# A forgetting-attention and feed-forward kernel: TensorE's order in the attention part written out by hand

## The chip, the cores and the metric

One core of one Trainium2 chip runs the whole program. The metric is the device time of one execution in microseconds (us). The kernel before took 1072.08 us, the median of three runs (1070.17 to 1072.96).

## The reference

Attention with a forget gate over 4 batches, 8 heads, 576 positions and 64 columns per head, then two feed-forward blocks over the 2304 tokens:

```python
scores = scale * np.matmul(q, k.transpose(0, 1, 3, 2))
cum = np.cumsum(np.log(np.clip(f, 0.0001, 1.0)), axis=-1)
scores = np.where(causal, -1e9, scores + cum[..., :, None] - cum[..., None, :])
attn = softmax(scores)
x = merge_heads(np.matmul(attn, v))                  # 2304 x 512
h = x @ w_in                                         # 512 -> 2048
x = (h * np.tanh(softplus(h))) @ w_out               # 2048 -> 512
out = ((x @ w1) * (x @ w2)) @ w3 @ w_out2            # 512 -> 1024 -> 1024 -> 512
```

## The kernel before

**Layout.** The 32 heads are worked on as 16 pairs; the two heads of a pair lie on the lower and the upper 64 partitions. The kernel multiplies `w3 @ w_out2` once into one weight (`wp`). Weights come in as 64-bit words and are turned into fp32 by a conversion job: one load (`cv_load`, SP's queue), one ScalarE instruction (`cv_exp`, L127), three VectorE instructions (`cv_bits`, L135 to L137), and then either a split into a high and a low part (`cv_split`: ScalarE L92, GpSimd L106) or a store (`cv_store`). There are 62 such jobs in the slots described below: 14 for w3 (slots 0 to 18), 16 for w_in (from slot 20, one a slot) and 32 for w_out, w1 and w2 (from slot 40). A large product of two split operands takes three matmuls (`MM_PAIRS`).

**One pair.** A pair has 576 query rows, cut into units c = 0 to 4: c = 0 to 3 are 128 rows of both heads against the first 128(c+1) keys, c = 4 is the last 64 rows of both heads together. Per unit:

- `scores` (L339 for c < 4, L344 for c = 4): raw products in fp32 (each matmul appears as two records) plus one product that adds the decay (`aug`). For c < 4 the two heads use 64 rows of the array each and write two different PSUM banks. There are two score buffers, `ps_s`, of two banks each, taken in turn by `bank()`.
- `softmax_a`: VectorE's mask-and-reduce (L363; L369 and L370 for c = 4), then ScalarE's exponential (L373), one of each per head.
- `transposes` (L407, L411, L412) of the exponentials through TensorE into `ps_t`, and `pt_parts` (L422, L425, L426), the copies out: head 0 on ScalarE, head 1 on VectorE.

After the five units of pair p, `pv(p)` (L440) multiplies by V: 28 records, the two heads in the left and the right 64 columns of the array, into a score buffer. The row sums are inverted (`inv_sums`, `inv_rows` with one transpose, L388), stored and read back from DRAM as rows (`inv_load`, tile `R`), and `x_rows` (L448) multiplies the P V result by them; `x_parts` splits it into the two halves that the first layer reads.

**Slots and fillers.** The attention is written as slots, five per pair; slot s issues `scores(s)`, then the transposes of slot s-1 (`T_LAG`), and `pv` of the pair before stands in the third slot of each pair (`PV_AT`). Between them run single matmuls from a queue, the fillers: 192 of `wp` (L481, 128x512), then the first layer (L511, 128x288) of batches 0 to 2, 384 each; `run_filler` takes them in order, as soon as the weights they need are marked in `done`. How many each slot takes is worked out by `plan` from costs given in `slot_cost`, over the stretches `WP_END` and `L1_S`. The first layer of batch 3 and everything after it (L775, L795, L815) is `phase_b`; it has no attention work. All of its matmuls are 128x288.

**What sets the order on the engines.** The program gives dependencies and priorities (`high_priority`); a scheduler that models the engines' time then places every engine's instructions, TensorE's too. `issue_after` adds an order on one engine: each filler goes behind the latest score matmul (`self.pe`), the conversions behind the softmax of their slot. [...]

Of the kernel before, what the change touches and what calls it, by code (L numbers as in the profile page):

```python
# [24 lines left out]
TB = S // 2  # L25
# [8 lines left out]
KQ = 3 * S  # L34
LAST = 2 * S - 64

T_LAG = 1
PV_AT = 2
HB = 3
CV = 2  # L40
HP_L1 = 50
# [4 lines left out]
MID = 7  # L46
EARLY = 10
W3_STEP = 1.42
PRE = 6
WP_END = 28  # L50
W_IN_SLOT = 20
L1_BOTH = 10
W_IN_STEP = 1.0
W_OUT_SLOT = 40
W_OUT_STEP = 1.3
L1_S = (23, 43, 64, 86)

MM_PAIRS = ((0, 0), (0, 1), (1, 0))

# [11 lines left out]
class Kernel:  # L71
# [4 lines left out]
    def __init__(self, ctx, tc, qk, v, f, w_in, w_out, w1, w2, w3t, wo2, out_t):  # L76
        self.ctx, self.tc, self.nc = ctx, tc, tc.nc
        self.qk, self.v, self.f = qk, v, f
        words = [w.bitcast(I32) for w in (w_in, w_out, w1, w2, w3t, wo2)]
        self.w_in, self.w_out, self.w1, self.w2, self.w3t, self.wo2 = words  # L80
        self.out_t = out_t
        self.cv, self.done, self.owed = {}, set(), 0
        self.V = {}
        self.filler = deque()
        self.nl1 = 0
        self.pe = None
# [51 lines left out]

    def cv_split(self, key, hi, lo, hi_eng="act", lo_eng="pool"):
        self.split(self.cv.pop(key)[1], hi, lo, hi_eng, lo_eng)  # L140
        self.done.add(key)

    def cv_store(self, key, dst):
        self.nc.sync.dma_start(dst, self.cv.pop(key)[1])
# [180 lines left out]
        self.V[p] = self.va  # L325


    def scores(self, s):
        p, c = divmod(s, NU)
        mm = self.nc.tensor.matmul  # L330
        ps = self.S[s] = self.bank()
        raw, aug = self.raw[p % 2], self.aug[p % 2]
        if c < 4:
            n = 128 * (c + 1)
            for t, first in ((raw, True), (aug, False)):
                for hh in range(2):
                    r = slice(64 * hh, 64 * hh + 64)
                    q0 = (2 * S + 64 if hh else S) + 128 * c
                    ins = mm(ps[:, 512 * hh:512 * hh + n], t[r, q0:q0 + 128], t[r, 0:n],  # L339
                             start=first, stop=not first)  # L340
            return ins
        for t, first in ((raw, True), (aug, False)):
            for part in range(2):
                ins = mm(ps[:, 512 * part:512 * part + TB], t[:, LAST:LAST + 128], t[:, TB * part:TB * part + TB],  # L344
                         start=first, stop=not first)
        return ins

    def softmax_a(self, s):
        p, c = divmod(s, NU)
        nc = self.nc  # L350
        ps = self.S.pop(s)
        if c == 0:
            self.sums = self.att.tile([128, 16], F32, name=f"sum{p}", tag="sum", bufs=2)
        ttr = nc.vector.tensor_tensor_reduce
        self.nsm = self.nsm % 6 + 1
        st = [self.sums[:, 8 + self.nsm:9 + self.nsm]]
        if c < 4:
            n = 128 * (c + 1)
            P = [self.P[(2 * s + hh) % 4] for hh in range(2)]
            self.nsm = self.nsm % 6 + 1  # L360
            st.append(self.sums[:, 8 + self.nsm:9 + self.nsm])
            for hh in range(2):
                ttr(P[hh][:, :n], ps[:, 512 * hh:512 * hh + n], self.m1[:, 512 - n:], -0.125, 3.0e38, ALU.add,  # L363
                    ALU.min, st[hh])
            cols = (c, 5 + c)
        else:
            n = S
            P = [self.P[2 * s % 4]]
            ttr(P[0][:, :TB], ps[:, :TB], self.m1[:, :TB], -0.125, 3.0e38, ALU.add, ALU.min, self.sums[:, 15:16])  # L369
            ttr(P[0][:, TB:n], ps[:, 512:512 + TB], self.m4, -0.125, self.sums[:, 15:16], ALU.add, ALU.min, st[0])  # L370
            cols = (4,)
        for t, b, i in zip(P, st, cols):
            ins = nc.scalar.activation(t[:, :n], t[:, :n], AF.Exp, bias=b, scale=-1.0, accum_out=self.sums[:, i:i + 1])  # L373
        return ins
# [25 lines left out]
    def transposes(self, s):  # L400
        p, c = divmod(s, NU)
        tr = self.nc.tensor.transpose
        if c < 4:
            for hh in range(2):
                P = self.P[(2 * s + hh) % 4]
                for k in range(c + 1):
                    tr(self.ps_t[hh][:, 128 * k:128 * k + 128], P[:, 128 * k:128 * k + 128], self.ident)  # L407
            return
        P = self.P[2 * s % 4]
# [4 lines left out]
    def pt_parts(self, s, hh):  # L414

        p, c = divmod(s, NU)
        nc = self.nc
        copy = nc.vector.tensor_copy if hh else nc.scalar.copy
        dst = self.pt[:, 2 * (p % 2) + hh]
        if c < 4:  # L420
            src = self.ps_t[hh][:, :128 * (c + 1)].rearrange("p (k q) -> p k q", q=128)
# [115 lines left out]
        return out  # L537


    @staticmethod  # L540
    def slot_cost(s):
        t = 0
        if s < NU * NPAIR:
            c = s % NU
            t += (300, 590, 880, 1170, 1320)[c]
        if 0 <= s - T_LAG < NU * NPAIR:
            t += (220, 440, 660, 880, 470)[(s - T_LAG) % NU]
        if s >= NU and s % NU == PV_AT:
            t += 2950
        return t  # L550

    def run_filler(self, n):

        self.owed += n
        while self.owed and self.filler and all(k in self.done for k in self.filler[0][0]):
            with self.behind(self.pe):
                self.filler.popleft()[1]()
            self.owed -= 1

    def behind(self, ins):  # L560
# [2 lines left out]

    def plan(self):

        last = NU * NPAIR + NU
        cnt = [0] * last
        segs = [(0, WP_END, 8 * 24 - PRE, 231)] + [(L1_S[i], min(L1_S[i + 1], last), 384, 132) for i in range(3)]
        for a, z, n, c in segs:
            cost = [self.slot_cost(s) for s in range(a, z)]  # L570
            lo, hi = 0.0, 1e6
            for _ in range(60):
                t = (lo + hi) / 2
                if sum(max(0.0, t - x) for x in cost) < n * c:
                    lo = t
                else:
                    hi = t
            acc, done = 0.0, 0
            for s, x in zip(range(a, z), cost):
                acc += max(0.0, lo - x) / c  # L580
                k = min(n, int(acc + 0.5)) - done
                cnt[s] = k
                done += k
        return cnt

    def phase_a(self):
# [31 lines left out]
            if i + EARLY < len(first):  # L618
                self.cv_load(first[i + EARLY][0], first[i + EARLY][1], where[i + EARLY])

        for i in range(7):
            go(i)
        self.filler.extend(self.wp_unit(0))
        self.run_filler(PRE)
        for i in range(7, 10):
            go(i)

        misc, conv = {}, {}
# [34 lines left out]
        for f in range(1, 8):  # L663
            self.filler.extend(self.wp_unit(f))
        cnt = self.plan()
        nslot = NU * NPAIR
        self.S, self.nsm = {}, 0
        act = dve = None
        for s in range(nslot + NU):
# [3 lines left out]
            with self.tc.high_priority(offset=HP_ATT):  # L673
                if s < nslot:
                    self.pe = self.scores(s)
                if 0 <= s - T_LAG < nslot:
                    self.transposes(s - T_LAG)
                    act = self.pt_parts(s - T_LAG, 0)
            if s < nslot:
                with self.tc.high_priority(offset=HP_SM):  # L680
                    act = self.softmax_a(s)
            with self.behind(act):
# [4 lines left out]
            if 0 <= s - T_LAG < nslot:  # L687
                with self.tc.high_priority(offset=HP_ATT):
                    dve = self.pt_parts(s - T_LAG, 1)
            with self.behind(dve):  # L690
                for key in conv.get(s, []):
                    self.cv_bits(key)
            with self.behind(act):
                for fn, a in misc.get(s, []):
                    fn(*a)
            self.run_filler(n - k)
            if s >= NU and s % NU == PV_AT:
                with self.tc.high_priority(offset=HP_PV):
                    p = s // NU - 1
                    self.pv(p)  # L700
                    self.x_rows(p)
                    self.x_parts(p)
        self.run_filler(len(self.filler))
        self.psp.__exit__(None, None, None)
        self.attp.__exit__(None, None, None)
        self.lowp.__exit__(None, None, None)


    def late_pool(self):
# [221 lines left out]
```

## Time and profile before

| | |
|---|---|
| median of the runs | 1072.08 us |
| the profiled execution | 1066.5 us |
| its span, first to last instruction | 1064.7 us |
| TensorE matmul busy | 1015.1 us (95%) |
| TensorE weight load busy | 887.2 us (83%) |
| VectorE busy | 420.2 us (39%) |
| ScalarE busy | 374.6 us (35%) |
| GpSimd busy | 232.6 us (22%) |
| mean granted TensorE clock | 0.995 |

The profile is of one execution. A matmul's end is modelled in it, and the next one may start before that end, so the cost of a matmul is read from the start of one to the start of the next, and a busy TensorE need not be a TensorE at its peak. PE is TensorE's matmuls, PEld its weight loads, DVE VectorE, ACT ScalarE, POOL GpSimd, SP the engine whose queue issues all DMAs here. In the timeline a line is a run of like instructions: start, time until the last one's modelled end, engine, line, tile written and read, rows*columns of the array, operand, how many, and in brackets the idle time before it and what ended it.

### The profile page before, as it was taken

The numbers are of one execution on the slowest core, as the hardware profiler recorded it, in microseconds if no ns is written. First come the engines' busy times: TensorE is split into PE (matmuls) and PEld (weight loads), VectorE is DVE, ScalarE is ACT, GpSimd is POOL, SyncE is SP. The second block draws the span as 40 slices with busy tenths as digits, with TensorE's granted clock in tenths as the row PEclk, the third lists the DMA queues.
The fourth block names the chain that finished last, engine by engine and source line by source line (L and its number), as shares of the span: only waits on it lengthen the run. The fifth ranks groups of instructions, "written<-read, shape, count | busy, mean of one in ns | idle before, by whom it ended". The sixth has DMA issues, their size and how long they took to land.

```text
span 1064.7 us, 18244 instructions
## 1 busy us (share of the span) xinstructions
PE 1015.1 (95%) x6912; PEld 887.2 (83%) x6912; DVE 420.2 (39%) x1049; ACT 374.6 (35%) x987; POOL 232.6 (22%) x299
## 2 busy tenths in 40 slices
PE   1698899999999999999999999999999999999998
PEld 0465567767777767669999999999999999999998
DVE  6956565653445455532232222222232122322311
ACT  2655556554355444443453121121212121121111
POOL 4632223320010000001571221212122121222100
PEclk9999999999999999999999999999999999999999
DMA  6545556652665666556973111111112111111000
GB/s 203 159 144 150 163 166 183 191 168 73 200 202 171 192 188 192 172 166 200 358 216 120 47 55 40 45 48 49 56 40 56 35 50 51 46 53 37 12 24 23
DMA packets 101132, 126.27 MB, mean 119 GB/s; under 512 B 10324, under 2 KB 81380, under 8 KB 101044
## 3 DMA queue, kind: packets, MB, share of 16 engines
q1 hardware_dynamic: 101044, 125.10, 39.1%
q8 instruction: 54, 0.88, 0.4%
q14 instruction: 34, 0.28, 0.1%
HBM read 88.43 MB, written 36.54 MB: 117 GB/s over the span
## 4 chain that ended last, share of the span: by engine, by line
PE 85%; DMA 8%; DVE 4%; SPq 1%; ACT 1%; issue 1%; POOL 0%; ACTq 0%; DVEq 0%
PE ps_x L775 18%; PE ps_l L511 17%; PE ps_y L795 10%; PE ps_l L795 10%; PE ps_s L440 6%; PE ps_s L339 5%; PE ps_l L815 5%; PE ps_y L815 5%; PE ps_l L481 3%; PE ps_t L407 3%; DMA cvro<-in_wo_dram 2%; PE ps_s L344 2%; DMA cvri<-in_w_in_dram 1%; DMA R<-inv_scr 1%; DMA cvrt<-in_w3t_dram 1%
## 5 line engine op out<-in xcount | busy, mean ns | idle before, releaser
L511 PE MATMUL ps_l<-x,wi 128*128 128x288 f32 x1536 | 251.3, 306 | 2.6 <-ACT h L518 1.6
L511 PEld LDWEIGHTS ps_l<-x,wi 128*128 128x128 f32 x1536 | 213.2, 189 | 34.6 <-issue 23.6
L775 PE MATMUL ps_x<-g,wo 128*128 128x288 f32 x1536 | 215.4, 294 | 0.0
L775 PEld LDWEIGHTS ps_x<-g,wo 128*128 128x128 f32 x1536 | 207.3, 188 | 0.0
L106 POOL TENSOR_TENSOR g<-m,g 128x288 fp32r<-128x288 f32 x128 | 106.2, 830 | 376.0 <-DVE g L94 362.3
L757 ACT ACTIVATE m<-hl 128x288 f32<-128x288 f32 x128 | 56.9, 446 | 283.1 <-POOL g L106 281.5
L795 PE MATMUL ps_y<-x,w 128*128 128x288 f32 x768 | 106.8, 294 | 0.0
L795 PE MATMUL ps_l<-x,w 128*128 128x288 f32 x768 | 106.7, 294 | 0.0
L795 PEld LDWEIGHTS ps_y<-x,w 128*128 128x128 f32 x768 | 103.3, 188 | 0.0
L795 PEld LDWEIGHTS ps_l<-x,w 128*128 128x128 f32 x768 | 103.3, 188 | 0.0
L373 ACT ACTIVATE P<-P,sum 128x128 f32<-128x128 f32 (+2 forms) x144 | 84.0, 584 | 51.9 <-DVE sum L363 47.1
L363 DVE CUSTOM_DVE_ANT_0 P<-ps_s,m 128x128 f32<-128x128 f32 (+3 forms) x128 | 59.7, 486 | 97.5 <-PE ps_t L407 80.5
L106 POOL TENSOR_TENSOR x<-xx,x 128x288 fp32r<-128x288 f32 x32 | 27.2, 872 | 263.7 <-ACT x L92 208.7
L803 DVE TENSOR_TENSOR cs<-ps_y,cs 128x288 f32<-128x288 f32 x32 | 14.7, 458 | 170.9 <-PE ps_y L795 170.9
L94 DVE CAST g<-m 128x288 fp32r<-128x288 f32 x128 | 41.1, 322 | 101.4 <-PE ps_x L775 97.9
L440 PE MATMUL ps_s<-pt,va 128*64 128x320 f32 (+3 forms) x384 | 77.6, 395 | 0.0
L339 PE MATMUL ps_s<-raw 64*128 64x128 f32 (+3 forms) x256 | 65.6, 497 | 5.9 <-DMA raw<-in_qk_dram 5.2
L407 PE MATMUL ps_t<-ident,P 128*128 128x128 f32 x320 | 58.5, 284 | 2.6 <-DVE pt L422 1.4
L339 PE MATMUL ps_s<-aug 64*128 64x128 f32 (+3 forms) x128 | 40.1, 515 | 21.2 <-DVE cvo L135 21.2
L407 PEld LDWEIGHTS ps_t<-ident,P 128*128 128x128 f32 x320 | 38.1, 141 | 25.7 <-issue 11.5
L518 ACT COPY h<-ps_l 128x288 f32<-128x288 f32 x96 | 37.8, 394 | 54.8 <-PE ps_l L511 33.0
L815 PE MATMUL ps_y<-ab,wpl 128*128 128x288 f32 x384 | 52.1, 294 | 0.0
(117 smaller groups left out, 1114.5 us busy)
## 6 DMA issues: line engine op xcount, KB each, us to landing
hl<-h_scr SPq DMA_DIRECT2D x128, 144.0 KB
h_scr<-h SPq DMA_DIRECT2D x96, 144.0 KB
raw<-in_qk_dram SPq DMA_DIRECT2D x32, 288.0 KB
cvrt<-in_w3t_dram SPq DMA_DIRECT2D x16, 512.0 KB
cvri<-in_w_in_dram SPq DMA_DIRECT2D x16, 512.0 KB
cvru<-in_w_out_dram SPq DMA_DIRECT2D x16, 512.0 KB
cvrv<-in_w_dram SPq DMA_DIRECT2D x16, 512.0 KB
h_scr<-hst SPq DMA_DIRECT2D x32, 144.0 KB
```

What stands on the lines that cost most here:

```text
L94: nc.vector.tensor_copy(hi, raw)
L106: ins = self.nc.gpsimd.tensor_tensor(lo[..., c], raw[..., c], f32(hi[..., c]), ALU.subtract)
L339: ins = mm(ps[:, 512 * hh:512 * hh + n], t[r, q0:q0 + 128], t[r, 0:n], start=first, stop=not first)
L363: ttr(P[hh][:, :n], ps[:, 512 * hh:512 * hh + n], self.m1[:, 512 - n:], -0.125, 3.0e38, ALU.add, ALU.min, st[hh])
L373: ins = nc.scalar.activation(t[:, :n], t[:, :n], AF.Exp, bias=b, scale=-1.0, accum_out=self.sums[:, i:i + 1])
L407: tr(self.ps_t[hh][:, 128 * k:128 * k + 128], P[:, 128 * k:128 * k + 128], self.ident)
L440: mm(ps[64 * hh:64 * hh + 64, 256 + q:256 + q + w], lhs, rhs, start=i == 0, stop=i == len(plan) - 1)
L511: mm(o[:, :TB], w, x, start=i == 0, stop=i == 11)
L757: self.nc.scalar.activation(y, h, AF.Mish)
L775: ins = mm(self.xb(e), self.wo[f][:, 512 * a + 128 * e:512 * a + 128 * e + 128], g[:, TB * b:TB * b + TB], start=f == 0 and k == 0, stop=f ...
L795: mm(ps, self.w12[f, i][:, 512 * a + 128 * e:512 * a + 128 * e + 128], self.x2[e][:, TB * b:TB * b + TB], start=n == 0, stop=n == 11)
L815: nc.tensor.matmul(ps, self.wp[f][:, 512 * a + 128 * e:512 * a + 128 * e + 128], self.ab[f][:, TB * b:TB * b + TB], start=n == 0, stop=n = ...
```

## The change

`T_LAG`, `PV_AT`, `PRE` and `slot_cost` go. In the attention part TensorE's instructions keep the order in which the program writes them (`manual_schedule`); the other engines are still placed by the scheduler. A pair's five slots hold: scores of units 0 and 1; transposes of 0 and 1, then scores of 2 and 3; transposes of 2; transposes of 3, then scores of 4; transposes of 4, then P V of the pair before. Fillers follow in each slot, in two halves with the slot's small jobs between them, in the proportions of `SHARE` (24, 18, 12, 18, 24; 96 in each slot behind the last pair). A weight counts as ready only from the slot after the one that converted it (`fresh`). The steps of the inverted sums move one slot earlier, the six `wp` fillers ahead of the slots go into them, `P` buffers and the columns of `ps_t` are numbered by c, and the stretches of the fillers move.

```diff
-T_LAG = 1
-PV_AT = 2
-PRE = 6
-WP_END = 28
+WP_END = 26
-L1_S = (23, 43, 64, 86)
+L1_S = (26, 46, 66, 84)
+SHARE = (24, 18, 12, 18, 24)
...
     def cv_split(self, key, hi, lo, hi_eng="act", lo_eng="pool"):
         self.split(self.cv.pop(key)[1], hi, lo, hi_eng, lo_eng)
-        self.done.add(key)
+        self.fresh.add(key)
...
-            P = [self.P[(2 * s + hh) % 4] for hh in range(2)]
+            P = [self.P[(2 * c + hh) % 4] for hh in range(2)]
...
-            P = [self.P[2 * s % 4]]
+            P = [self.P[0]]
...
+    def t_col(c):
+        return 128 if c == 1 else 0
...
     def run_filler(self, n):
 
         self.owed += n
         while self.owed and self.filler and all(k in self.done for k in self.filler[0][0]):
-            with self.behind(self.pe):
-                self.filler.popleft()[1]()
+            self.filler.popleft()[1]()
             self.owed -= 1
...
-        segs = [(0, WP_END, 8 * 24 - PRE, 231)] + [(L1_S[i], min(L1_S[i + 1], last), 384, 132) for i in range(3)]
...
+        segs = [(0, WP_END, 8 * 24)] + [(L1_S[i], L1_S[i + 1], 384) for i in range(3)]
+        for a, z, n in segs:
+            share = [SHARE[s % NU] if s < NU * NPAIR else 96 for s in range(a, z)]
             acc, done = 0.0, 0
...
+                acc += n * x / sum(share)
...
-        for i in range(7):
-            go(i)
-        self.filler.extend(self.wp_unit(0))
-        self.run_filler(PRE)
-        for i in range(7, 10):
+        for i in range(10):
             go(i)
...
-            at(s + 4, self.inv_sums)
-            at(s + 5, self.inv_rows, p)
-            at(s + 6, self.inv_load, p)
+            at(s + 3, self.inv_sums)
+            at(s + 4, self.inv_rows, p)
+            at(s + 5, self.inv_load, p)
...
+        with self.tc.manual_schedule(engines={mybir.EngineType.PE}):
+            self.slots(misc, conv, self.plan())
...
+    def slots(self, misc, conv, cnt):
+
+        def turn(p, cs):
+            with self.tc.high_priority(offset=HP_ATT):
+                for c in cs:
+                    self.transposes(p, c)
+                for c in cs:
+                    self.act = self.pt_parts(p, c, 0)
+                    self.dve = self.pt_parts(p, c, 1)
+
+        def score(p, cs):
+            with self.tc.high_priority(offset=HP_SM):
+                for c in cs:
+                    self.scores(p, c)
+                for c in cs:
+                    self.act = self.softmax(p, c)
+
+        for s in range(NU * (NPAIR + 1)):
+            self.done |= self.fresh
+            self.fresh.clear()
             if s in L1_S[:3]:
                 self.filler.extend(self.l1_all(L1_S.index(s)))
+            p, j = divmod(s, NU)
             n = cnt[s]
...
+            live = p < NPAIR
+            if live:
+                if j == 0:
+                    score(p, (0, 1))
+                elif j == 1:
+                    turn(p, (0, 1))
+                    score(p, (2, 3))
+                elif j == 2:
+                    turn(p, (2,))
+                elif j == 3:
+                    turn(p, (3,))
+                    score(p, (4,))
+                else:
+                    turn(p, (4,))
+            if p and j == (4 if live else 2):
+                with self.tc.high_priority(offset=HP_PV):
+                    self.pv(p - 1)
+                    self.x_rows(p - 1)
+                    self.x_parts(p - 1)
+            with self.behind(self.act):
                 for key in conv.get(s, []):
                     self.cv_exp(key)
+            with self.behind(self.dve):
+                for key in conv.get(s, []):
+                    self.cv_bits(key)
             k = n // 2
             self.run_filler(k)
...
+            with self.behind(self.act):
                 for fn, a in misc.get(s, []):
                     fn(*a)
             self.run_filler(n - k)
```

## Rows read from the trace of the kernel before

**Rows 1.** Busy time by stretch: stretch, length, each engine, granted clock, DMA share, GB/s.
```profile
156.50:485.40 328.90, 324.95 (x1993) 236.26 (x1991) 166.50 (x438) 162.63 (x462) 44.59 (x54) 1.00 0.59 178
485.40:1064.70 579.30, 575.10 (x4342) 574.50 (x4341) 147.91 (x369) 132.79 (x328) 128.75 (x159) 1.00 0.24 73
```
**Rows 2.** The same view of line L511 alone (matmuls, weight loads).
```profile
181.20:439.70 258.50, 140.56 (x804) 113.07 (x804) 1.00 0.59 175
0.00:485.40 485.40, 181.15 (x1036) 145.62 (x1036) 0.99 0.58 173
```
**Rows 3.** The same view of line L481 alone.
```profile
50.50:156.50 106.00, 47.24 (x168) 30.21 (x168) 0.97 0.53 157
```
**Rows 4.** Timeline of TensorE, 224 to 226 us: part of one pair's P V.
```profile
224.73 0.75 PE L440 MATMUL ps_s<-pt,va 128*64 128x320 f32 x2
225.41 0.40 PE L511 MATMUL ps_l<-x,wi 128*128 128x288 f32 x1
225.74 0.75 PE L440 MATMUL ps_s<-pt,va 128*64 128x320 f32 x2
```
**Rows 5.** Timeline of TensorE: first and last score and P V piece, 181 to 440 us.
```profile
181.21 0.49 PE L339 MATMUL ps_s<-raw 64*128 64x128 f32 x4
...
192.23 1.41 PE L440 MATMUL ps_s<-pt,va 128*64 128x256 f32 x12
...
432.58 0.33 PE L440 MATMUL ps_s<-pt,vb 128*64 128x64 f32 x2
...
434.12 1.13 PE L339 MATMUL ps_s<-raw 64*128 64x512 f32 x4
```
**Rows 6.** Timeline of TensorE, 77 to 97 us: groups that run undivided, and what follows.
```profile
77.29 0.71 PE L407 MATMUL ps_t<-ident,P 128*128 128x128 f32 x5
77.83 1.14 PE L344 MATMUL ps_s<-raw 128*128 128x288 f32 x4
...
79.06 0.61 PE L481 MATMUL ps_l<-wo,w3h 128*128 128x512 f32 x2
...
80.51 0.49 PE L339 MATMUL ps_s<-raw 64*128 64x128 f32 x4
...
81.00 0.73 PE L481 MATMUL ps_l<-wo,w3h 128*128 128x512 f32 x2
...
90.99 1.30 PE L440 MATMUL ps_s<-pt,va 128*64 128x320 f32 x8
92.22 0.28 PE L388 MATMUL ps_t<-ident,sum 128*9 128x128 f32 x1
...
95.67 1.13 PE L339 MATMUL ps_s<-raw 64*128 64x512 f32 x4
...
96.96 0.73 PE L481 MATMUL ps_l<-wo,w3h 128*128 128x512 f32 x2
```
**Rows 7.** Timeline of TensorE, 60 to 62 us: three L481 matmuls in a row.
```profile
60.76 0.62 PE L481 MATMUL ps_l<-wo,w3h 128*128 128x512 f32 x2
...
61.44 0.62 PE L481 MATMUL ps_l<-wo,w3h 128*128 128x512 f32 x2
```
**Rows 8.** Timeline of TensorE, 50 to 54 us: pair 1 begins, and a wait.
```profile
50.49 0.49 PE L339 MATMUL ps_s<-raw 64*128 64x128 f32 x4
...
53.85 1.02 PE L481 MATMUL ps_l<-wo,w3h 128*128 128x512 f32 x2 [2.33 <-ACT w3h L92]
```
**Rows 9.** Groups by line and form, 181.2 to 439.7 us: busy us, mean ns, idle before.
```profile
L373 ACT ACTIVATE P<-P,sum 128x256 f32<-128x256 f32 x18 | 9.0, 504 | 0.7 <-DVE sum L363 0.7
...
L137 DVE SCALAR_TENSOR_TENSOR cvi<-cvri,cvi 128x512 int32<-128x512 int32 x10 | 7.9, 788 | 0.2
...
L363 DVE CUSTOM_DVE_ANT_0 P<-ps_s,m 128x256 f32<-128x256 f32 x18 | 6.9, 421 | 6.6 <-PE ps_t L411 5.1 <-PE ps_s L339 1.4
```
**Rows 10.** Timeline of TensorE at 102 us: a wait for the row factors.
```profile
102.01 2.29 PE L344 MATMUL ps_s<-raw 128*128 128x288 f32 x4 [3.17 <-DVE xx L448]
```
**Rows 11.** Waits, 50 to 485 us: engine, line, waited for: total us, times, longest us.
```profile
ACT cvi L127 <- DMA cvri<-in_w_in_dram: 10.9, 8, 2.7
```

More of the change, by code (lines that the diff above doesn't have):

```diff
@@ L81, in __init__ @@
         self.out_t = out_t
-        self.cv, self.done, self.owed = {}, set(), 0
+        self.cv, self.done, self.fresh, self.owed = {}, set(), set(), 0
         self.V = {}
@@ L325, in load_v, with scores @@
         self.V[p] = self.va
-    def scores(self, s):
-        p, c = divmod(s, NU)
+    def scores(self, p, c):
         mm = self.nc.tensor.matmul
-        ps = self.S[s] = self.bank()
+        ps = self.S[p, c] = self.bank()
         raw, aug = self.raw[p % 2], self.aug[p % 2]
@@ L338, in scores, with softmax @@
                     q0 = (2 * S + 64 if hh else S) + 128 * c
-                    ins = mm(ps[:, 512 * hh:512 * hh + n], t[r, q0:q0 + 128], t[r, 0:n],
-                             start=first, stop=not first)
-            return ins
+                    mm(ps[:, 512 * hh:512 * hh + n], t[r, q0:q0 + 128], t[r, 0:n], start=first, stop=not first)
+            return
         for t, first in ((raw, True), (aug, False)):
             for part in range(2):
[L344 to L349, printed above, removed]
+                mm(ps[:, 512 * part:512 * part + TB], t[:, LAST:LAST + 128], t[:, TB * part:TB * part + TB],
+                   start=first, stop=not first)
+    def softmax(self, p, c):
         nc = self.nc
-        ps = self.S.pop(s)
+        ps = self.S.pop((p, c))
         if c == 0:
@@ L398, in inv_load, with transposes @@
         self.nc.sync.dma_start(self.R[64:128, 512:], d[:, S:640].broadcast_to([64, 64]))
-    def transposes(self, s):
-        p, c = divmod(s, NU)
+    @staticmethod
+    def t_col(c):
+        return 128 if c == 1 else 0
+    def transposes(self, p, c):
         tr = self.nc.tensor.transpose
         if c < 4:
+            o = self.t_col(c)
             for hh in range(2):
-                P = self.P[(2 * s + hh) % 4]
+                P = self.P[(2 * c + hh) % 4]
                 for k in range(c + 1):
-                    tr(self.ps_t[hh][:, 128 * k:128 * k + 128], P[:, 128 * k:128 * k + 128], self.ident)
+                    tr(self.ps_t[hh][:, o + 128 * k:o + 128 * k + 128], P[:, 128 * k:128 * k + 128], self.ident)
             return
-        P = self.P[2 * s % 4]
+        P = self.P[0]
         for k in range(4):
@@ L412, in transposes, with pt_parts @@
         tr(self.ps_t[1][0:64, 0:128], P[:, 512:576], self.ident)
-    def pt_parts(self, s, hh):
-        p, c = divmod(s, NU)
+    def pt_parts(self, p, c, hh):
         nc = self.nc
@@ L420, in pt_parts @@
         if c < 4:
-            src = self.ps_t[hh][:, :128 * (c + 1)].rearrange("p (k q) -> p k q", q=128)
+            o = self.t_col(c)
+            src = self.ps_t[hh][:, o:o + 128 * (c + 1)].rearrange("p (k q) -> p k q", q=128)
             return copy(dst[:, 0:c + 1, 128 * c:128 * c + 128], src)
@@ L537, in l1_all @@
         return out
[L540 to L550, printed above, removed]
     def run_filler(self, n):
@@ L564, in plan @@
     def plan(self):
-        last = NU * NPAIR + NU
+        last = NU * (NPAIR + 1)
         cnt = [0] * last
-        segs = [(0, WP_END, 8 * 24 - PRE, 231)] + [(L1_S[i], min(L1_S[i + 1], last), 384, 132) for i in range(3)]
[L569 to L577, printed above, removed]
+        segs = [(0, WP_END, 8 * 24)] + [(L1_S[i], L1_S[i + 1], 384) for i in range(3)]
+        for a, z, n in segs:
+            share = [SHARE[s % NU] if s < NU * NPAIR else 96 for s in range(a, z)]
             acc, done = 0.0, 0
-            for s, x in zip(range(a, z), cost):
-                acc += max(0.0, lo - x) / c
+            for s, x in zip(range(a, z), share):
+                acc += n * x / sum(share)
                 k = min(n, int(acc + 0.5)) - done
@@ L661, in phase_a @@
                     at(s + 1, self.load_cum, 2 * p + 2 + hh)
-        for f in range(1, 8):
+        for f in range(8):
             self.filler.extend(self.wp_unit(f))
[L665 to L669, printed above, removed]
+        self.S, self.nsm, self.act, self.dve = {}, 0, None, None
+        with self.tc.manual_schedule(engines={mybir.EngineType.PE}):
+            self.slots(misc, conv, self.plan())
@@ new lines, in phase_a @@
+        self.psp.__exit__(None, None, None)
+        self.attp.__exit__(None, None, None)
+        self.lowp.__exit__(None, None, None)
+    def slots(self, misc, conv, cnt):
[15 more added lines that the diff above has]
+            self.fresh.clear()
@@ L670, in phase_a @@
             if s in L1_S[:3]:
                 self.filler.extend(self.l1_all(L1_S.index(s)))
+            p, j = divmod(s, NU)
             n = cnt[s]
[L673 to L681, printed above, removed]
@@ L682, in phase_a @@
-            with self.behind(act):
+            live = p < NPAIR
[17 more added lines that the diff above has]
+                    self.x_parts(p - 1)
@@ L683, in phase_a @@
+            with self.behind(self.act):
                 for key in conv.get(s, []):
                     self.cv_exp(key)
+            with self.behind(self.dve):
+                for key in conv.get(s, []):
+                    self.cv_bits(key)
             k = n // 2
             self.run_filler(k)
[L687 to L692, printed above, removed]
@@ L693, in phase_a @@
-            with self.behind(act):
+            with self.behind(self.act):
                 for fn, a in misc.get(s, []):
@@ L696, in phase_a @@
             self.run_filler(n - k)
[L697 to L702, printed above, removed]
         self.run_filler(len(self.filler))
-        self.psp.__exit__(None, None, None)
-        self.attp.__exit__(None, None, None)
-        self.lowp.__exit__(None, None, None)
     def late_pool(self):
```

## The prediction, on record before the changed kernel ran

> **What bounds the kernel now.** I read the busy time by stretch first. From 485.4 us on, when the last P V is done, TensorE issues 4342 plain matmuls in 579.3 us, 0.133 us each, with its weight loads as busy as its matmuls [rows 1]. Nothing in that part is touched, so the question is when TensorE gets there. Before it, too, TensorE is shown busy nearly throughout (325.0 of 328.9 us), while VectorE and ScalarE are at half (166.5 and 162.6 us) [rows 1]. But a busy TensorE is not an efficient one. In the nine pairs from 181.2 to 439.7 us there are 804 first-layer matmuls [rows 2]. At 0.133 us they need 106.9 of the 258.5 us, which leaves 151.6 us, or **16.8 us per pair**, for scores, transposes and P V. From 50.5 to 156.5 us there are 168 fillers of the 512-wide kind [rows 3]; three of these take 0.68 us, 0.227 us each [rows 7], so 38.1 us, and the other 67.9 us go to about 4.1 pairs, 16.5 us each.
>
> Next I read the timeline of TensorE, once where the work is broken up and once where it is not. Broken up: two P V records of 320 columns, one head's alone, and one first-layer matmul repeat every 1.01 us [rows 4]; the other head's records come in the next piece, though its half of the array was free. Counted over that timeline, the nine pairs hold 59 pieces of half-row scores and 75 pieces of P V; the first and last of each are [rows 5]. Undivided groups are far cheaper, from their start to the start of what follows [rows 6]: scores of 128 columns 0.49 us, of 512 columns 1.29 us, hence 0.27 us for each 128 columns on top of 0.22 us once per visit, and about 0.75 and 1.02 us for 256 and 384; unit 4 1.23 us; five transposes 0.54 us; eight P V records of 320 columns 1.23 us.
>
> **The undivided price of a pair.** Scores of units 0 and 1 as one group: 0.49 + 0.75 - 0.22 = 1.02 us; of 2 and 3: 1.02 + 1.29 - 0.22 = 2.09 us. Unit 4: 1.23 us. 25 transposes at 0.108 us: 2.7 us. P V: 1600 columns per head in two records each; the 1.23 us less 0.1 us for the change of columns are 0.88 ns per record column, so 3200 of them side by side take 2.8 us, and 2.9 us with the change back. For entering three groups I add 0.1 us each, an estimate. Sum **10.2 us**, against 16.8 and 16.5 us now. The gain has two sources: fewer visits, and heads that run side by side again instead of one after the other. [...]
>
> [...] The trace agrees: of the 1.01 us [rows 4], two records of one head at 0.88 ns a column take 0.56 us and the filler 0.13, which leaves 0.32 us per visit. [...]
>
> **Waits, the unknown term.** In the written order TensorE stands still when an exponential is late, and the fillers behind it stand too; the scheduler had put something ready there. Nothing shows these waits, so I bound them. After scores of 0 and 1, four reductions and four exponentials must end before the next slot's transposes. With about 0.42 us a reduction and 0.5 us an exponential [rows 9], plus each one's reading of the sum, and starting as unit 0's scores end, I estimate 3.2 us. The cover is unit 1's scores (0.53 us) and the slot's fillers: 24 x 0.133 = 3.2 us while a batch of the first layer takes 20 slots; nine of the wide ones, 2.1 us, ahead of slot 26; some 14, 1.9 us, in slots 66 to 79, where the four slots behind the last pair take 228 of 384. For unit 4 I estimate 2.2 us against 2.4, 1.6 and 1.4 us. The turns of units 2 and 3 have over 0.5 us to spare. So nominally no wait in eight pairs and about 1.4 us per pair elsewhere. A conversion that has just started adds up to 0.79 us on VectorE [rows 9]. Lower bound 0 per pair; upper bound 5.2 us, each of four turns late by one VectorE conversion and one exponential, 1.3 us. I take **2 us per pair**, nearer the lower end, because both engines are half idle [rows 1].
>
> **Edits that cost nothing, with their cover.** The inverted sums move a slot earlier while P V moves two slots later, so the three row loads, which pass SP's queue ahead of the next slot's weight load, have some four slots to land. Today TensorE waits 3.17 us for them at 102 us [rows 10], and such waits go. Their transpose now has 2.9 us of P V before it, which covers ScalarE's and VectorE's work on the sums. If that cover failed it would be 0.5 us per pair. x of a batch's last pair is written in slot 24, 44 or 64, and first read two slots later. A weight usable one slot later (`fresh`) takes away waits on weights that are only just issued; w3's units keep up to two slots of lead. The six early fillers move behind the first scores, where VectorE's conversions set the pace anyhow. DMA's share is 0.59 before 485.4 us [rows 1]; squeezed by a sixth it is 0.7, and I price that at nothing.
>
> **The sum, against the profiled execution (1066.5 us).**
> - Slot 5 (pair 1) starts at 50.5 us now [rows 8]. By the new order 36 fillers must be done by then, 12 of them on the second unit, whose weights arrive at 53.85 us [rows 8]; plus the fourth slot's nine fillers: 56 us, 5.5 us later than now.
> - Slots 5 to 25, 4.2 pairs: 155 x 0.227 = 35.2, 4.2 x 10.2 = 42.8, waits 8.4: to 142.4 us.
> - Slots 26 to the last P V (slot 82): 768 + 156 + 114 = 1038 first-layer matmuls, as many as today's 1036 at that point [rows 2]: 138.1; 10.8 pairs x 10.2 = 110.2; the last P V 2.9; waits 21.6: to 415.2 us.
>
> Today that point is 485.4 us, so **70 us are saved**: 996 us by the profiled execution. That one stands 5.6 us under the median of the runs, 1072.08 us; taken from the median, **1002 us**. With the two ends for the waits (0 and 5.2 us, 15 pairs) this becomes 972 and 1050 us.
>
> **The rivals.**
> 1. *Every turn is late* (12%): waits at the upper bound. For: four turns a pair, and conversions that meet each of them. Against: half-idle engines. 1050 us.
> 2. *Only the visits are saved, the heads overlap no better* (10%): 14.9 visits a pair (134 pieces in nine pairs [rows 5]) become 3; 11.9 x 0.32 = 3.8 us instead of 6.6, so 2.8 us x 15 = 42 us are missing: 1044 us. Against it: the undivided rows, which are measured.
> 3. *The order does not come out as written* (4%): conversions are late ahead of slot 26, fillers are owed and bunch up, and the turns there stand bare, some 7 us of lost cover for 4.2 pairs: about 1031 us.
> 4. *Slower* (6%): ScalarE's list holds `cv_exp` in front of exponentials; when its load has not landed, all behind it are late, and TensorE, which can no longer do something else, with them. Now such waits reach 2.7 us and cost TensorE nothing [rows 11]. 62 jobs x 2.7 us = 167 us against 100 us of gain without waits: 1139 us. It decides from 1.6 us a job. For it: slots become a fifth shorter, so loads have less time. Against: only 8 such waits are shown for w_in's 16 jobs.
>
> [...]
>
> **How the numbers follow.** My forecast has 68%, with its own range 972 to 1042 us. Rivals 2 and 3 lie inside; 970 to 1045 leaves out rivals 1 and 4 and a little of the forecast's ends, 2 in 10 together. About 0.3%, 3.2 us, is what a measurement can tell: faster by more than that 0.91 (forecast, rivals 2 and 3, most of 1), within it 0.03 (the tail of rival 1, waits still longer), slower 0.06.
>
> **What would show it.** P V as one run of 28 records per pair lasting about 2.9 us; scores of two units in one run of 1.0 and 2.1 us; the last P V ending near 415 us, and 579 us from there to the end as now; waits on TensorE named after the exponential (L373), about 2 us per pair, most in the transposes of units 0, 1 and 4. I am wrong if the groups run undivided and still cost over 13 us, if waits exceed 5 us per pair, or if the stretch behind the last P V grows, because phase B's weights or its first activations are not there in time.

## The result, and the profile after

The changed kernel takes **1012.96 us** (median of 4 runs, 1009.55 to 1016.22) against 1072.52 us for the kernel before on the same chip: a ratio of **0.9446 [0.9406, 0.9487]**. In lines of the changed kernel, scores are L336 (unit 4 L340), reductions L357 and L363, exponentials L367, transposes L405 and L409, the copies behind them L420, P V L438, `wp` fillers L479, first-layer matmuls L509, their evacuation L516.

From the head of the page, one profiled execution of 1015.13 us:

```profile
PE 947.8 (94%) x6912; PEld 875.3 (86%) x6912; DVE 420.4 (41%) x1049; ACT 367.7 (36%) x987; POOL 241.1 (24%) x299
```

Busy time by stretch, columns as in [rows 1]: slots 5 to 25, pairs 6 to 14, the last pair up to the end of the last P V, and what follows it.

```profile
59.80:154.30 94.50, 83.82 (x504) 59.30 (x504) 64.09 (x167) 55.63 (x157) 33.27 (x39) 0.98 0.58 176
175.96:388.20 212.24, 204.26 (x1555) 174.18 (x1554) 126.41 (x343) 120.38 (x360) 32.59 (x35) 1.00 0.68 204
388.20:433.90 45.70, 40.51 (x284) 34.77 (x283) 20.25 (x50) 21.25 (x57) 5.89 (x7) 0.93 0.71 224
433.90:1013.30 579.40, 574.90 (x4338) 574.03 (x4338) 146.42 (x366) 131.75 (x327) 128.61 (x159) 1.00 0.24 71
```

The same view of L509 alone:

```profile
175.96:388.20 212.24, 117.70 (x797) 107.75 (x796) 1.00 0.68 204
0.00:433.90 433.90, 155.78 (x1039) 143.06 (x1039) 0.98 0.65 196
```

What to see: the part behind the last P V is as long as before, 579.4 against 579.3 us [rows 1], and as many first-layer matmuls are done ahead of it, 1039 against 1036 [rows 2]. So the whole gain lies ahead of the last P V, which now ends at 433.9 us instead of 485.4: 51.5 us. Weight loads are now busy for 174.2 of the 212.2 us of pairs 6 to 14 (82%); before it was 236.3 of the 328.9 us from 156.5 us to the last P V (72%) [rows 1].

TensorE's timeline from pair 8's first scores to pair 9's:

```profile
224.51 0.49 PE L336 MATMUL ps_s<-raw 64*128 64x128 f32 x4
...
225.60 3.44 PE L509 MATMUL ps_l<-x,wi 128*128 128x288 f32 x24
228.88 0.82 PE L405 MATMUL ps_t<-ident,P 128*128 128x128 f32 x6
229.63 0.92 PE L336 MATMUL ps_s<-raw 64*128 64x384 f32 x4
...
231.74 2.68 PE L509 MATMUL ps_l<-x,wi 128*128 128x288 f32 x18
234.26 0.82 PE L405 MATMUL ps_t<-ident,P 128*128 128x128 f32 x6
234.83 1.83 PE L509 MATMUL ps_l<-x,wi 128*128 128x288 f32 x12
236.50 1.03 PE L405 MATMUL ps_t<-ident,P 128*128 128x128 f32 x8
237.37 1.14 PE L340 MATMUL ps_s<-raw 128*128 128x288 f32 x4
...
238.60 2.55 PE L509 MATMUL ps_l<-x,wi 128*128 128x288 f32 x18
240.99 0.60 PE L409 MATMUL ps_t<-ident,P 128*128 128x128 f32 x4
...
241.63 2.81 PE L438 MATMUL ps_s<-pt,va 128*64 128x256 f32 x24
244.27 0.28 PE L438 MATMUL ps_s<-pt,vb 128*64 128x64 f32 x4
244.48 1.88 PE L509 MATMUL ps_l<-x,wi 128*128 128x288 f32 x12
...
248.02 0.49 PE L336 MATMUL ps_s<-raw 64*128 64x128 f32 x4
```

From start to start: scores 225.60 - 224.51 = 1.09 and 231.74 - 229.63 = 2.11 us; transposes 0.75, 0.57, 0.87 and 0.64, 2.83 us together; unit 4 238.60 - 237.37 = 1.23; P V 244.48 - 241.63 = 2.85; with 0.03 us for the inverted sums' transpose **10.14 us**. The P V is one visit of 28 records; before, nine pairs had 75 pieces of it [rows 5]. Pairs 6 to 14 have 797 fillers; at 0.133 us they are 106.0 of the 212.2 us, which leaves 11.8 us a pair where it was 16.8.

### The profile page after: what moved, and what is told of

Its sections match the earlier page's. It is cut to its first block, busy times and chain, and to the rows that moved or that the text cites. A ratio compares the mean times of both kernels' runs of the same rounds, so it can differ in the third digit from the quotient of the medians.

```text
span 1013.3 us, 18304 instructions
## 1 busy us (share of the span) xinstructions
PE 947.8 (94%) x6912; PEld 875.3 (86%) x6912; DVE 420.4 (41%) x1049; ACT 367.7 (36%) x987; POOL 241.1 (24%) x299
## 4 chain that ended last, share of the span: by engine, by line
PE 71%; DMA 5%; DVE 2%; ACT 2%; SPq 1%; issue 1%; POOL 1%; ACTq 0%; DVEq 0%
PE ps_x L770 19%; PE ps_l L509 14%; PE ps_y L790 10%; PE ps_l L790 10%; PE ps_l L810 5%; PE ps_y L810 5%; PE ps_s L438 3%; PE ps_s L336 2%; DMA wor<-wo_scr 1%; PE ps_t L405 1%; DMA cvrv<-in_w_dram 1%; DMA wo_scr<-cvu 1%; ACT P L367 1%; DMA w_scr<-cvv 1%; POOL wo L104 1%
## 5 line engine op out<-in xcount | busy, mean ns | idle before, releaser
L509 PE MATMUL ps_l<-x,wi 128*128 128x288 f32 x1536 | 225.5, 302 | 3.9 <-ACT h L516 2.8
L509 PEld LDWEIGHTS ps_l<-x,wi 128*128 128x128 f32 x1536 | 210.2, 191 | 15.2 <-issue 7.2
L367 ACT ACTIVATE P<-P,sum 128x128 f32<-128x128 f32 (+2 forms) x144 | 83.1, 579 | 52.8 <-DVE sum L357 36.0
L357 DVE CUSTOM_DVE_ANT_0 P<-ps_s,m 128x128 f32<-128x128 f32 (+3 forms) x128 | 56.7, 485 | 22.1 <-PE ps_s L336 21.3
L516 ACT COPY h<-ps_l 128x288 f32<-128x288 f32 x96 | 37.4, 392 | 56.7 <-PE ps_l L509 42.7
L336 PE MATMUL ps_s<-aug 64*128 64x128 f32 (+3 forms) x128 | 36.5, 554 | 22.7 <-DVE cvo L133 22.6
L336 PE MATMUL ps_s<-raw 64*128 64x128 f32 (+3 forms) x256 | 50.0, 472 | 6.2 <-DMA raw<-in_qk_dram 5.7
L405 PE MATMUL ps_t<-ident,P 128*128 128x128 f32 x320 | 46.0, 281 | 10.4 <-ACT pt L420 6.5
L405 PEld LDWEIGHTS ps_t<-ident,P 128*128 128x128 f32 x320 | 37.8, 144 | 16.9 <-ACT pt L420 9.4
L810 PE MATMUL ps_l<-ab,wpl 128*128 128x288 f32 x384 | 52.1, 294 | 0.0
```

The costliest lines, as they stand in the source:

```text
L405: tr(self.ps_t[hh][:, o + 128 * k:o + 128 * k + 128], P[:, 128 * k:128 * k + 128], self.ident)
L509: mm(o[:, :TB], w, x, start=i == 0, stop=i == 11)
L516: self.nc.scalar.copy(t, o[:, :TB])
L810: nc.tensor.matmul(ps, self.wp[f][:, 512 * a + 128 * e:512 * a + 128 * e + 128], self.ab[f][:, TB * b:TB * b + TB], start=n == 0, stop=n = ...
```

## The experiments

The kernel before took 1065 to 1073 us in the median on the chips used, so kernels are compared by their ratio to it on the same chip. Experiments 1 to 4 are one profiled execution each; beside them the kernel before took 1065.48 us.

**1. The heads one after the other.** P V undivided, but in each of its two accumulations all of one head first.

```diff
-            for i, (kc, q, w) in enumerate(plan):
-                for hh in range(2):
+            for hh in range(2):
+                for i, (kc, q, w) in enumerate(plan):
```

> The changed kernel, but P V takes all of head 0 and then all of head 1, still in one undivided visit. Theory (half of the gain in P V is that the two heads run side by side): P V goes from 2.85 us to about 5.5 us a pair, 16 pairs, +42 us, about 1055 us. Rival (only the number of visits counts): P V stays at 2.9 us and the time at 1013 us.

The time is 1030.46 us. P V of the pair at 249 us, and what follows it, in the timeline of TensorE:

```profile
249.06 2.81 PE L438 MATMUL ps_s<-pt,va 128*64 128x256 f32 x17
...
253.58 1.89 PE L509 MATMUL ps_l<-x,wi 128*128 128x288 f32 x12
```

4.52 us instead of 2.85: 1.67 more a pair, 27 us in 16 pairs, of which some 20 reach the time (changed kernel: 0.948 x 1065.48 = 1010 us). P V is two accumulations, one behind the other: 8 records over 256 and 128 columns, then 20 over 320, 192 and 64. Busy time of L438 alone over the first one, in this kernel and in the changed one:

```profile
249.06:249.76 0.70, 0.70 (x8) 0.57 (x9) 1.00 0.82 228
241.63:242.32 0.69, 0.69 (x8) 0.55 (x10) 1.00 0.53 184
```

The first accumulation takes 0.70 us, 0.69 in the changed kernel: by its time its heads still ran side by side, although the program writes all of one head ahead of the other. Only the second one came apart, 3.82 us (249.76 to 253.58) instead of 2.15, and even there the other head's first 320-column record, the last of the 17 above, starts before the first head's last 64-column ones (251.70, 251.76). So heads side by side are worth something, against rival 2, and at least 1.67 us a pair; the 2.8 us a pair that I had put on it is neither shown nor refuted, since this edit parts the heads only in the second accumulation. The expected time was a miss.

**2. P V broken by fillers, heads kept together.** One filler after each step of both heads, taken from the slot's own share.

```diff
                     mm(ps[64 * hh:64 * hh + 64, 256 + q:256 + q + w], lhs, rhs, start=i == 0, stop=i == len(plan) - 1)
+                if kc < 4:
+                    self.run_filler(1)
...
                     self.pv(p - 1)
+                    n -= 6
```

> The changed kernel, but one filler between the seven steps of P V, the heads still paired: six more visits a pair, the same number of fillers in all. Theory (a visit costs 0.32 us by itself): +1.9 us a pair, +31 us, about 1043 us. Rival (a break costs only when it parts the heads): within 5 us of 1013 us.

The time is 1038.94 us, 29 us above 1010, as expected. TensorE's timeline:

```profile
229.60 0.76 PE L438 MATMUL ps_s<-pt,va 128*64 128x320 f32 x4
230.29 0.40 PE L511 MATMUL ps_l<-x,wi 128*128 128x288 f32 x1
230.62 0.76 PE L438 MATMUL ps_s<-pt,va 128*64 128x320 f32 x4
```

The period is 1.01 us, the same as in the kernel before; but it holds four records, two of each head, where it held two of one head [rows 4]. So two more records fit into the same 1.01 us, those of the other head: its half of the array was unused in the kernel before. A pair costs 12.8 us besides its fillers at 0.133, against 10.7 for the undivided one: 2.0 us for six more visits, **0.33 us each** (0.32 forecast from [rows 4]).

**3. The new slots without the kept order.** The slots stay, the scheduler is free to move TensorE's instructions.

```diff
-        with self.tc.manual_schedule(engines={mybir.EngineType.PE}):
-            self.slots(misc, conv, self.plan())
+        self.slots(misc, conv, self.plan())
```

> The changed kernel without the one call that keeps TensorE's order: the scheduler places TensorE again, over the new slots. Theory (the gain is in the order being kept): groups break up again, over 10 visits a pair, 1055 to 1075 us. Rival (the new slots alone bring the groups together): 3 to 5 visits a pair, 1010 to 1025 us.

The time is 1033.46 us, a miss: between the theories. TensorE's timeline:

```profile
274.60 0.40 PE L509 MATMUL ps_l<-x,wi 128*128 128x288 f32 x1
274.83 0.27 PE L410 MATMUL ps_t<-ident,P 128*64 128x128 f32 x1
275.03 0.54 PE L438 MATMUL ps_s<-pt,va 128*64 128x192 f32 x2
```

P V falls apart again, into 7 to 10 pieces in pairs 7 to 14. The score groups nearly hold: four visits a pair, 3.54 us. So the rest of the change by itself mends the scores, and P V stays whole only where the order is kept.

**4. The kept order alone.** The kernel before, its slot loop under `manual_schedule` and nothing else of the change. Run again in experiment 7, beside the changed kernel.

```diff
-        for s in range(nslot + NU):
+        with self.tc.manual_schedule(engines={mybir.EngineType.PE}):
+            for s in range(nslot + NU):
```

> The kernel before, its slots and shares unchanged, but TensorE keeps the order written there: four score groups and one P V group a pair. Theory (keeping the order is most of the gain, the regrouping a small part): five visits a pair, scores about 0.5 us dearer a pair than in the changed kernel, more waits since a unit's transposes come one short slot after its scores: 1020 to 1045 us. Rival (the new grouping is what counts): above 1055 us.

The time is 1011.04 us, a clear miss: the grouping that I held to be worth 10 us and more is worth nothing beside the kept order. One pair's TensorE timeline, 243 to 258 us (the pair's first two score groups stand ahead of it):

```profile
243.89 0.92 PE L339 MATMUL ps_s<-raw 64*128 64x384 f32 x4
...
244.91 0.66 PE L407 MATMUL ps_t<-ident,P 128*128 128x128 f32 x4
245.33 0.51 PE L511 MATMUL ps_l<-x,wi 128*128 128x288 f32 x2
245.77 2.81 PE L440 MATMUL ps_s<-pt,va 128*64 128x256 f32 x24
...
248.62 1.13 PE L339 MATMUL ps_s<-raw 64*128 64x512 f32 x4
...
249.92 0.88 PE L407 MATMUL ps_t<-ident,P 128*128 128x128 f32 x6
250.55 2.76 PE L511 MATMUL ps_l<-x,wi 128*128 128x288 f32 x19
```

P V is undivided, 248.62 - 245.77 = 2.85 us. Summed over the pair from start to start, scores are 3.55 us in four visits (3.20 in two after), transposes 2.55 (2.83 after), P V and unit 4 the same: 10.2 us against 10.1. What is saved by merging scores is lost in the transposes, by what stands behind them: in the changed kernel's timeline above six of them take 0.75 us ahead of half-row scores (228.88 to 229.63) and 0.57 us ahead of fillers (234.26 to 234.83), and the last five 0.64 us ahead of P V, where 0.52 us do ahead of a filler in this kernel. Six transposes ahead of fillers take 0.63 us in this kernel (249.92 to 250.55), where half-row scores stand in front of them, so the neighbour in front counts too. That the price of entering a half-array group is then paid in the transposes fits these rows; no run isolates it.

**5. Unit 4's scores one slot earlier, and a shorter tail.** Two kernels. In the changed kernel the largest group of waits of TensorE stands in front of unit 4's transposes (waits, 0 to 430 us: engine, tile, line, waited for, total us, times, longest):

```profile
PE ps_t L409 <- ACT P L367: 15.8, 13, 2.5
PE ps_t L405 <- ACT pt L420: 6.5, 6, 1.7
```

How one of them comes about, VectorE's timeline at 286 us; unit 4's scores start at 284.59, and its transposes at 289.12, after a wait of 0.74 us:

```profile
285.88 0.68 DVE L420 COPY pt<-ps_t 128x512 f32<-128x512 f32 x1
286.48 0.68 DVE L135 SCALAR_TENSOR_TENSOR cvu<-cvru,cvu 128x512 int32<-128x512 int32 x1
287.08 0.45 DVE L363 CUSTOM_DVE_ANT_0 P<-ps_s,m 128x288 f32<-128x288 f32 x1
```

The reduction L363 waits behind a copy and a conversion. The first kernel gives it a slot more (the transposes stay where they are), the second takes fillers out of the slots behind the last pair:

```diff
                     turn(p, (2,))
+                    score(p, (4,))
                 elif j == 3:
                     turn(p, (3,))
-                    score(p, (4,))
```
```diff
-            share = [SHARE[s % NU] if s < NU * NPAIR else 96 for s in range(a, z)]
+            share = [SHARE[s % NU] if s < NU * NPAIR else 48 for s in range(a, z)]
```

> The changed kernel, but the scores of unit 4 stand one slot earlier, behind the transposes of unit 2. Theory (the waits in front of unit 4's transposes, 15.8 us in the changed kernel, are softmax work that has too few fillers in front of it): these waits fall under 4 us, nothing else grows, 1001 to 1006 us. Rival (VectorE and ScalarE are late whatever stands in between, the wait moves to unit 3's transposes): within 3 us of 1013 us, with the waits under another unit's name.

> The changed kernel with a share of 48 instead of 96 in the slots behind the last pair, so pairs 13 to 15 get some 81 fillers each instead of 57. Theory (short slots leave the turns there without cover, 1.5 to 3 us a pair, and the long tail gains nothing): 1006 to 1010 us, non-filler time of pairs 13 and 14 down to 12 us. Rival (the same waits come back behind the last P V, where fewer fillers are left to wait for the last x): no change within 3 us, a wait on x (L90 or L104) in the tail.

Medians of four runs: the first 994.91 us, ratio **0.9334 [0.93, 0.9368]**; the second 1002.6 us, 0.9407 [0.9373, 0.9441], against 0.948 [0.9456, 0.9504] for the changed kernel (experiment 7). The row of the first that answers to L409's, 50 to 440 us:

```profile
PE ps_t L409 <- ACT P L367: 0.8, 3, 0.4
```

The waits before unit 4 go from 15.8 to 0.8 us, and those on the copy L420, in front of unit 3's transposes, from 6.5 to 1.0. Against the theory other waits grow, by some 4.5 us in all up to 440 us. By the ratios the time falls by some 15.6 us, more than the 7 to 12 us expected. The second kernel lies some 7.8 us under the changed one by the ratios, where 3 to 7 us were expected. Of this second kernel the stretch from the start of the last pair to the end of the last P V, columns as in [rows 1]:

```profile
387.40:424.10 36.70, 35.80 (x275) 31.02 (x274) 19.02 (x48) 20.70 (x56) 5.85 (x7) 1.00 0.82 270
```

162 fillers in 36.7 us, where the changed kernel has 170 in 45.7 at a granted clock of 0.93. Some of that is moved, not saved: pairs 13 and 14 carry the fillers instead, and have 11.1 us each left over besides them, where they had 12.0 and 13.4.

**6. The kept order with the old grouping, and no wait on weights.** Experiment 4's kernel waits 11.1 us for w3's conversions in its first slots (below, waits, 30 to 440 us); its pair 1 starts at 70.7 us, in the changed kernel at 59.8. Taken over from the change: `fresh`, and the early `wp` fillers put into the slots.

```profile
PE ps_l L481 <- ACT w3h L92: 11.1, 4, 3.3
```
```diff
-        self.done.add(key)
+        self.fresh.add(key)
...
-        for i in range(7):
+        for i in range(10):
             go(i)
         self.filler.extend(self.wp_unit(0))
-        self.run_filler(PRE)
-        for i in range(7, 10):
-            go(i)
...
+                self.done |= self.fresh
+                self.fresh.clear()
```

> The kernel before with TensorE's order kept, as in old_manual, and with the one-slot delay for new weights and no fillers ahead of the slots, as in the changed kernel. Theory (in old_manual TensorE waits 15.5 us for weights that are being converted, all ahead of 80 us, and the delay puts other fillers first): these waits fall under 5 us and the time is 1000 to 1007 us. Rival (conversions set the pace at the start in either case, so slots start as late): within 3 us of old_manual's 1011 us.

The median of four runs is 996.07 us, ratio 0.9349 [0.9312, 0.9385]; pair 1 at 60.4 us; the row that answers to it:

```profile
PE ps_l L481 <- ACT w3h L92: 2.7, 1, 2.7
```

Neither part of the theory came out as put: the time fell further than to 1000 us, and the waits on weights (this row, and the rows for L106 and for `wo`) went from 15.5 to 7.3 us, not under 5. Slot 10, where pair 2 starts, comes at 79.8 us instead of 94.8, so nearly the whole gain lies ahead of it, and the waits are 8.2 us of these 15. The granted clock rose there as well, from 0.83 to 0.93 (means over the 50 us below), which by my estimate makes up part of the rest; busy time of 40 to 90 us, columns as in [rows 1], experiment 4's kernel first:

```profile
40.00:90.00 50.00, 38.41 (x168) 24.17 (x168) 25.45 (x60) 19.02 (x52) 15.16 (x18) 0.83 0.30 94
40.00:90.00 50.00, 46.41 (x252) 30.94 (x251) 35.91 (x91) 29.77 (x82) 19.04 (x24) 0.93 0.51 149
```

Both groupings, each with its own large wait mended, come to the same time. That the wait, together with the lower granted clock beside it (0.83 here; 0.50 from 143.80 to 147.20 us in the changed kernel, behind a wait of 2.48 us), is what held either of them back fits this; `fresh` and the moved early fillers were not tried apart.

**7. Repeats on one chip, and both mends of experiment 5 together.** No edit for the first; experiment 4's kernel for the second.

> The changed kernel unaltered, beside the next two on one chip. By the ratio measured already (0.9446) it should lie at 0.940 to 0.949 of the kernel before.

> The kernel before with TensorE's order kept and nothing else, timed this time. Theory (keeping the order is the whole gain; the new grouping saves 0.35 us of scores a pair and gives 0.3 us back in transposes): within 0.5% of the changed kernel, ratio to the kernel before 0.940 to 0.950. Rival (the single look flattered it, the grouping is worth 5 us or more): ratio above 0.950.

> Both edits together: scores of unit 4 a slot earlier, and 48 as the share behind the last pair. Theory (they mend different waits, the one in front of unit 4, the other the short slots of pairs 13 to 15): 3 to 5 us under the earlier scores alone, ratio 0.928 to 0.932. Rival (with the earlier scores the short slots have cover enough): 0.933 to 0.935.

Medians of four or five runs: changed kernel 1011.23 us, 0.948 [0.9456, 0.9504]; kept order alone 1012.95 us, 0.9489 [0.9466, 0.9512]; both mends 994.4 us, 0.9319 [0.93, 0.9337]. The first two are the same, as expected. The shorter tail adds nothing that can be told once unit 4's scores are earlier: the ratio lies where the theory put it, but 1.6 us under the earlier scores alone and not 3 to 5, and its interval reaches into the rival's. Either version of 0.93 beats both kernels by some 15 us or more; between the two the runs do not decide.

## Why the prediction was right, and where it missed

The forecast was 1002 us, a ratio of 0.935; 0.9446 was measured, inside the range. By its steps:

- **The undivided price of a pair**: 10.2 us forecast, 10.14 measured, each part within 0.15 us (no run shows the 0.1 us for entering a group, or for P V's change of columns, by itself; above their forecasts lie the scores by 0.07 and 0.02 us and the transposes by 0.13, 2.83 us for 2.7), with the P V as one run of 28 records and scores of 1.09 and 2.11 us. The visit at 0.32 us held too (0.33, experiment 2). Rival 2 falls: its place, the heads' overlap, is shown by the period in experiment 2, though experiment 1, which parts the heads only in the second accumulation, shows 1.67 us a pair of the 2.8.
- **Where the gain comes from** is half as I put it. Fewer visits and heads side by side are both shown. But I took the rewritten slots for their cause; the kept order alone gives the whole of the gain (experiments 4 and 7), and the slots without it give a little over half (experiment 3: 32 of some 55 us).
- **Behind the last P V**: nothing changes, as forecast (579.4 us). The matmuls done ahead of it, 1039, are the 1038 forecast.
- **The waits, the term that was mis-sized.** The last P V was to end at 415.2 us and ends at 433.9, 18.7 us later. The forecast of a wait in front of units 0, 1 and 4 named the right engine and, for unit 4, the right place; but it spread 2 us evenly over 15 pairs, and it knew no cost of a wait beyond itself. Taken apart: (a) slot 5 starts at 59.80, 3.8 us late; two exponentials are waited for ahead of it, 2.1 and 1.9 us, which I had not counted there. (b) Slots 5 to 25 take 94.5 us, not 86.4. In pairs 1 to 4 some 14.5 us are not fillers at 0.227 us, 4.3 above the price where I took 2: the waits marked there come to 10.6 us instead of 8.4, of which 4.5 are in front of unit 3's transposes and wait for the copy L420, where the prediction saw 0.5 us to spare, a P V took 4.05 us for its 24 records instead of 2.81, 2.53 us of it at a granted clock of 0.50, and most of the rest is fillers that cost over 0.227 us each (the 146 of these pairs take 37.2 us, waits left out, where 33.1 was forecast). (c) Pairs 6 to 14 leave 11.8 us, 1.6 above the price: less than 2, worth 3.6 us. (d) The last pair and what stands behind it take 45.7 us; its 170 fillers are 22.6, which leaves 23.1 where 10.2 + 2.9 + 2 was to do, 8 us more. The waits marked there are 5.2 us instead of 2, and some 2 us are the clock's (below); some 3 us are not accounted for. The starts (a), the short slots (b) and the tail (d) less the gain of (c) and a further 2 us in the rest of pair 5 give the 18.7.
- **Why the miss in the median is smaller**: the profiled execution of before stood 5.6 us below the median of its runs, that of after stands 2.2 us above. By profiled executions the miss is 1015.1 - 996 = 19 us, by medians 11; that the two differ is chance, not a merit of the forecast.
- **Edits that cost nothing**: the 3.17 us wait for row factors [rows 10] is gone; 0.5 us of its kind is left. DMA's share rose from 0.59 to 0.68 in pairs 6 to 14, as forecast (0.7), with no transfer shown to hold TensorE there.
- **Rival 1**, every turn late by 1.3 us, does not come: pairs 8 and 9 have 10.7 us besides their fillers, hardly more than the price. **Rival 3** does not come either: the groups ahead of slot 26 come in the written order, six stretches of fillers a pair. **Rival 4** was to decide from 1.6 us for each of 62 jobs; all the waits marked on TensorE from slot 5 to the last P V come to some 25 us, so it is off by its size. Its mechanism does appear, in the tail (below).

The wait of 2.48 us before unit 4's transposes at 143.59 us is followed by a granted clock of 0.50 from 143.80 to 147.20 us, and one of 2.09 us at 411.98 us by 0.50 from 413.50 to 420.30. TensorE's timeline there:

```profile
143.59 0.94 PE L409 MATMUL ps_t<-ident,P 128*128 128x128 f32 x4 [2.48 <-ACT P L367]
...
144.67 4.05 PE L438 MATMUL ps_s<-pt,va 128*64 128x256 f32 x24
...
411.98 2.10 PE L509 MATMUL ps_l<-x,wi 128*128 128x288 f32 x12 [2.09 <-ACT h L516]
...
414.79 16.25 PE L509 MATMUL ps_l<-x,wi 128*128 128x288 f32 x102 [0.71 <-ACT h L516]
```

The 102 matmuls in 16.25 us would take 13.6 at 0.133. The repeat of the changed kernel in experiment 7 ran the tail at a granted clock of 1.00, with a wait of 2.08 us in the same place, and took 2 us less for them:

```profile
413.18 14.19 PE L509 MATMUL ps_l<-x,wi 128*128 128x288 f32 x102 [0.92 <-ACT h L516]
```

So what follows a long wait can cost on top of it, and the sum has no term for that. In the kernel before, unit 4's four raw matmuls behind the 3.17 us wait take 2.29 us [rows 10], at a granted clock of 0.50 from 102 to 104 us, and 1.14 us at 77.83 us [rows 6]. The two stretches at 0.50 above follow a wait too, but the repeat kept a granted clock of 1.00 behind one as long, so the gap alone does not settle it.

Why the evacuation L516 comes late in the tail can be read from ScalarE's timeline:

```profile
408.89 0.67 ACT L125 ACTIVATE cvv<-cvrv 128x512 f32<-128x512 f32 x1 [3.56 <-DMA w_scr<-cvv]
409.57 1.28 ACT L752 ACT_TABLE_LOAD   x1
...
411.55 0.38 ACT L516 COPY h<-ps_l 128x288 f32<-128x288 f32 x1
```

A conversion (L125) ahead of it in ScalarE's list waits 3.56 us for the store of an earlier one, and a table load (1.28 us) and two activations of phase B come in between. That is rival 4's mechanism, with a store in place of a load, once and not 62 times. No run changes that order, so it is read and not tested.

What stays open: the 3 us of the tail that nothing marked accounts for, and why the granted clock was 0.50 behind one wait of 2.09 us and 1.00 behind the other, of 2.08.

## What to carry to other kernels

Where groups use half of the array, look at what stands between their pieces in the timeline: a filler there costs a visit, here 0.33 us, and can part two halves that would run side by side (here 1.01 us for two records of one head, and for four of both). Keeping TensorE's written order is worth trying by itself before rewriting the order; what it exposes are the waits that the scheduler had filled, so read the waits next and give the latest one a slot more (here some 15 us for one moved line). Price such waits by the place, where fillers are few and where they end, rather than as one mean.

## What was not expected of the hardware

What stood behind a group of transposes went with a part of its cost: six took 0.57 us ahead of full-array fillers and 0.75 us ahead of a half-row group (0.63 us with half-row scores in front and fillers behind). Where one group of half-row work was joined to another, some of the visit that was saved turned up in front of it: 2.83 against 2.55 us of transposes a pair, for 3.20 against 3.55 us of scores. With all of one head written ahead of the other, P V's first accumulation, of 8 records, still ran its heads side by side (0.70 us), and only the second, of 20, came apart (3.82 us for 2.15). And behind a wait of 2.1 us in the tail the same kernel had a granted clock of 0.50 for 6.8 us in one execution, and of 1.00 in another.
